# Batch normalisation after a three-tap convolution: the second batch's input transform moved between the first unit's products, with loads and last stores reordered

## Chip, cores and metric

The kernel runs on one core of a Trainium2 chip. The metric is the device time of one execution in microseconds; the median of three runs before the change is 204.71 us (204.09 to 204.76). Engines are named as the profile names them: PE is TensorE, DVE VectorE, ACT ScalarE, POOL GpSimd and SP SyncE, whose queue issues the DMAs.

## What is computed

```python
B, S, C = 2, 2048, 1024      # x is (B, S, C), w is (3, C, C), all bf16

def reference(x, w, mean, var, g, b):
    K, P = 3, 1
    xp = jnp.pad(x, ((0, 0), (P, P), (0, 0)))
    y = sum(jnp.einsum('bsc,cd->bsd', xp[:, k:k + S, :], w[k]) for k in range(K))
    inv_std = 1.0 / jnp.sqrt(var + 1e-5)
    y = (y - mean) * (g * inv_std) + b
    return jax.nn.silu(y)
```

It is a convolution over the sequence with three taps and 1024 channels in and out, then a scale and a shift for each channel and silu.

## The kernel before

**The algorithm.** Six outputs along the sequence are made from eight inputs with eight products per channel pair instead of eighteen (a Winograd form). The sequence of 2048 gives 342 tiles of six outputs (NTB). For each of the eight positions j (NJ) there is a transformed input `T_sb[bi][:, ct, j, :]` and a transformed weight; positions 0 and 7 use the raw slices w[0] and w[2], positions 1 to 6 use sums of the three slices.

**Input transform (L201 to L242).** The sequence is cut into 17 windows of 21 tiles (the last has 6), for each batch. A window's load is 256 KB (L214; the first one of a batch is two DMAs into `xw0`, L210 and L211). Eight matmuls (L224) multiply it by the small matrix `Rm`, four into each of two groups of PSUM; there are four groups of two banks, used in turn (`next_group`). Each group is evicted as bf16 into `T_sb` by ACT (L236) or DVE (L238), chosen by a running sum of costs. `Rm` is made at the start by DVE (L93) and POOL (L105). All 34 windows are done before the first product. The load of the first weights and of the parameters (L183) is issued by SP after the load of window 1; the second column block's weights are loaded after window 20, the third's after the last window.

**Weights.** For each column block dc of 128 output channels, three slices are loaded (L130), scaled by 4, 4 and 2 (L140 on DVE for the first, L142 on ACT for the others) and combined by nine POOL operations of 128x1024 (L153 to L161) into one tile `uch`. The transposed parameters `prmT` (PE L188, DVE L189) give `beta` and `sk` on POOL (L191 to L197).

**Units (L287 to L361).** A unit is one column block of one batch: 16 units. Each has 64 products (L263) of 128x128 by 128x342, eight for each of eight banks, in the order of positions 1 to 6, 0, 7. ACT copies three banks into SBUF (`Ac`, L305, L308, L309), DVE makes the sums and differences and the six outputs `y[i]` (L266, L316 to L331), ACT applies silu with scale and bias into `yT` (L296), one transposing DMA turns `yT` to rows (L340) and five stores write it (L269). Silus and stores of a unit are issued within the next unit (`late_a`, `late_b`): ACT's order is three silus, copy 0, three silus, copies 1 and 2, scalings. The last unit is transposed by PE (L356), copied by DVE and ACT (L358, L360) and stored block by block, in five stores.

**What sets the order.** The schedule is manual: on each engine instructions run in the order in which the program issues them, and an instruction that waits holds all behind it on its engine. SP issues all DMAs in one order.

Of the kernel before, what the change touches and what calls it, by code (L numbers as in the profile page):

```python
# [8 lines left out]
ACT = mybir.ActivationFunctionType  # L9
# [26 lines left out]
def kernel(  # L36
# [28 lines left out]
    upool = ctx.enter_context(tc.tile_pool(name="upool", bufs=3))  # L65
    wtmp = ctx.enter_context(tc.tile_pool(name="wtmp", bufs=1))
    pspool = ctx.enter_context(tc.tile_pool(name="ps", bufs=1, space=bass.MemoryType.PSUM))

    ps_all = pspool.tile([P, 8 * 512], FP32, name="ps_all")

    dummy = consts.tile([P, 2], FP32, name="dummy")
    nc.vector.memset(dummy, 0.0)
    nc.scalar.activation(dummy[:, 1:2], dummy[:, 0:1], ACT.Silu)

# [3 lines left out]
    nc.gpsimd.iota(val, pattern=[[-1, NJ], [-M_OUT, WT]], base=0, channel_multiplier=1)  # L78
    E = consts.tile([P, NJ, WT], FP32, name="E")
# [34 lines left out]
    xw0 = consts.tile([P, C], BF16, name="xw0")  # L114
    nc.gpsimd.memset(xw0[0:1, :], 0.0)
    ident = consts.tile([P, P], BF16, name="ident")
    make_identity(nc, ident)
# [6 lines left out]
    w_all = w.rearrange("k (ct p) d -> p k ct d", p=P)  # L124
    raw, wts = {}, {}

    def load_weights(dc):
        wch = wpool.tile([P, 3, CT, P], BF16, name="wch")
        for k in (2, 0, 1):
            nc.sync.dma_start(out=wch[:, k], in_=w_all[:, k, :, dc * P:(dc + 1) * P])  # L130
        raw[dc] = wch

    def scale_weights(dc, first=False):
        wch = raw[dc]
        w1x2 = wtmp.tile([P, CT, P], BF16, name="w1x2")
        w0x4 = wtmp.tile([P, CT, P], BF16, name="w0x4")
        w2x4 = wtmp.tile([P, CT, P], BF16, name="w2x4")
        for dst, k, f in ((w2x4, 2, 4.0), (w0x4, 0, 4.0), (w1x2, 1, 2.0)):
            if first:
                nc.vector.tensor_scalar(dst, wch[:, k], f, 0.0, op0=ALU.mult, op1=ALU.add)  # L140
            else:
                nc.scalar.mul(dst, wch[:, k], f)  # L142
        return w1x2, w0x4, w2x4

    def transform_weights(dc, scaled):
        wch = raw[dc]
        w1x2, w0x4, w2x4 = scaled
        uch = upool.tile([P, 6, CT, P], BF16, name="uch")
        e1 = wtmp.tile([P, CT, P], FP32, name="e1")
        e2 = wtmp.tile([P, CT, P], FP32, name="e2")  # L150
        eh = wtmp.tile([P, CT, P], FP32, name="eh")
        w0, w1, w2 = wch[:, 0], wch[:, 1], wch[:, 2]
        nc.gpsimd.tensor_tensor(e1, w0, w2, op=ALU.add)  # L153
        nc.gpsimd.tensor_tensor(uch[:, 0], e1, w1, op=ALU.add)  # L154
        nc.gpsimd.tensor_tensor(uch[:, 1], e1, w1, op=ALU.subtract)  # L155
        nc.gpsimd.tensor_tensor(e2, w0, w2x4, op=ALU.add)  # L156
        nc.gpsimd.tensor_tensor(uch[:, 2], e2, w1x2, op=ALU.add)  # L157
        nc.gpsimd.tensor_tensor(uch[:, 3], e2, w1x2, op=ALU.subtract)  # L158
        nc.gpsimd.tensor_tensor(eh, w0x4, w2, op=ALU.add)  # L159
        nc.gpsimd.tensor_tensor(uch[:, 4], eh, w1x2, op=ALU.add)  # L160
        nc.gpsimd.tensor_tensor(uch[:, 5], eh, w1x2, op=ALU.subtract)  # L161
        wts[dc] = (wch, uch)

    T_sb = [tpool.tile([P, CT, NJ, NTB], BF16, name=f"T_sb{bi}") for bi in range(B)]
    CH = 4
    grp_i = 0
    eng_load = {"act": 0.0, "dve": 1.0}
    EVAC_COST = {"act": 0.75, "dve": 0.80}

    def next_group():  # L170
        nonlocal grp_i
        gi = grp_i % 4
        grp_i += 1
        return ps_all[:, gi * 1024:(gi + 1) * 1024].rearrange("p (s e) -> p s e", e=256)

    prm = consts.tile([4 * DC, P], BF16, name="prm")
# [3 lines left out]

    def load_params():
        for q, ap in enumerate((var, g, mean, b)):
            nc.sync.dma_start(out=prm[q * DC:(q + 1) * DC, :], in_=ap.rearrange("(dc p) -> dc p", p=P))  # L183

    def make_params():
        grp = next_group()
        pv = grp[:, 0, 0:2 * DC].bitcast(BF16)
        nc.tensor.transpose(pv, prm, ident[0:4 * DC, 0:4 * DC])  # L188
        nc.vector.tensor_copy(prmT.rearrange("p q d -> p (q d)"), pv)  # L189
        rstd = consts.tile([P, DC], FP32, name="rstd")  # L190
        nc.gpsimd.tensor_scalar(rstd, prmT[:, 0, :], 1e-5, 1.0, op0=ALU.add, op1=ALU.mult)  # L191
        nc.gpsimd.tensor_tensor(rstd, rstd, mhalf, op=ALU.pow)
        sc = consts.tile([P, DC], FP32, name="sc")
# [5 lines left out]
    win_i = 0  # L199
    with tc.tile_pool(name="xwin", bufs=12) as xpool:  # L200
        for bi in range(B):  # L201
            for wi in range(NWIN):
                ntile = min(WT, NTB - WT * wi)
                n0 = WT * wi
                t_lo = M_OUT * n0 - 1
                t_hi = min(t_lo + M_OUT * ntile + 1, S - 1)
                kk = t_hi - t_lo + 1
                if t_lo < 0:
                    xw = xw0
                    nc.sync.dma_start(out=xw[1:113, :], in_=x[bi, 0:112, :])  # L210
                    nc.sync.dma_start(out=xw[113:kk, :], in_=x[bi, 112:t_hi + 1, :])  # L211
                else:
                    xw = xpool.tile([P, C], BF16, name="xw")
                    nc.sync.dma_start(out=xw[0:kk, :], in_=x[bi, t_lo:t_hi + 1, :])  # L214
                if win_i == 1:
                    load_weights(0)
                    load_params()
                if win_i == 20 and DC > 1:
                    load_weights(1)
                for h in range(CT // CH):  # L220
                    grp = next_group()
                    for c4 in range(CH):
                        ct = h * CH + c4
                        nc.tensor.matmul(  # L224
                            grp[:, c4, 0:NJ * ntile],
                            lhsT=xw[0:kk, ct * P:(ct + 1) * P],
                            rhs=Rm[0:kk, :, 0:ntile],
                            start=True,
                            stop=True,
                        )  # L230
                    src = grp[:, :, 0:NJ * ntile].rearrange("p s (j n) -> p s j n", j=NJ)
                    dst = T_sb[bi][:, h * CH:(h + 1) * CH, :, n0:n0 + ntile]
                    eng = min(eng_load, key=lambda e: eng_load[e] + EVAC_COST[e])
                    eng_load[eng] += EVAC_COST[eng]
                    if eng == "act":
                        nc.scalar.copy(dst, src)  # L236
                    else:
                        nc.vector.tensor_copy(dst, src)  # L238
                if win_i == 3:
                    scaled = scale_weights(0, first=True)  # L240
                    make_params()
                    transform_weights(0, scaled)  # L242
                win_i += 1
    if DC > 2:
        load_weights(2)

    epool = ctx.enter_context(tc.tile_pool(name="epool", bufs=1))
    opool = ctx.enter_context(tc.tile_pool(name="opool", bufs=2))

    out_f = out.flatten_outer_dims()  # L250
    bank = [ps_all[:, i * 512:i * 512 + NTB] for i in range(8)]


    def mms(bk, j, dc, bi):
        wch, uch = wts[dc]
        for ct in range(CT):
            if j == 0:
                lhsT = wch[:, 0, ct, :]
            elif j == 7:
                lhsT = wch[:, 2, ct, :]  # L260
            else:
                lhsT = uch[:, j - 1, ct, :]
            nc.tensor.matmul(bank[bk], lhsT=lhsT, rhs=T_sb[bi][:, ct, j, :], start=(ct == 0), stop=(ct == CT - 1))  # L263
# [4 lines left out]
    def store(dst, src):  # L268
        nc.sync.dma_start(out=dst, in_=src)  # L269

    def store_block(o_v, dc, bi, nb):
# [5 lines left out]
        cuts = [n0, n1] if (n1 - n0) % 16 == 0 else [n0, n1 - (n1 - n0) % 16, n1]  # L277
        for c0, c1 in zip(cuts, cuts[1:]):
            dst = out_f[r0 + c0 * M_OUT:r0 + c1 * M_OUT, dcols].rearrange("(n i) d -> n i d", i=M_OUT)
            store(dst, o_v[c0 - n0:c1 - n0])  # L280
        if nb == NB - 1 and S % M_OUT:
            dst = out_f[r0 + full * M_OUT:r0 + S, dcols].rearrange("(n i) d -> n i d", i=S % M_OUT)
            store(dst, o_v[full - n0:full - n0 + 1, 0:S % M_OUT])

    units = [(dc, bi) for dc in range(DC) for bi in range(B)]
    late_a, late_b = [], []
    for ui, (dc, bi) in enumerate(units):  # L287
        last = ui == len(units) - 1
        yT = yTs[ui % 2]
# [3 lines left out]
        y = [epool.tile([P, NTB], FP32, name=f"y{i}") for i in range(M_OUT)]  # L293

        def silu(i, yT=yT, y=y, dc=dc):
            nc.scalar.activation(  # L296
                yT[:, i, 0:NTB], y[i], ACT.Silu, bias=beta[:, dc:dc + 1], scale=sk[:, dc:dc + 1]
            )
# [93 lines left out]
```

## Time and profile before

| what | us |
| --- | --- |
| median of three runs | 204.71 |
| the profiled execution | 205.36 |
| its span, first to last instruction | 203.6 |
| first input matmul starts | 4.34 |
| first product starts (unit 0) | 39.82 |
| unit 1 starts on PE | 49.10 |
| last product ends | 190.95 |

Busy time of the engines in stretches of the span (core 0, us):

| stretch | PE | DVE | ACT | POOL | DMA GB/s |
| --- | --- | --- | --- | --- | --- |
| 0 to 10 | 2.99 | 4.17 | 3.62 | 4.06 | 198 |
| 10 to 20 | 9.56 | 8.97 | 7.05 | 6.25 | 329 |
| 20 to 30 | 6.84 | 7.08 | 6.44 | 9.92 | 278 |
| 30 to 40 | 9.11 | 8.96 | 8.73 | 9.84 | 288 |
| 100 to 120 | 19.80 | 18.58 | 12.97 | 19.69 | 155 |
| 190 to 204 | 3.95 | 7.13 | 4.50 | 0.00 | 117 |

Busy time is the union of an engine's instructions in the stretch. Idle time is listed with what ended it: an instruction's own releaser, taken from semaphores. A timeline row merges neighbouring instructions of one line: start, duration, engine, line, operation, output<-input, count, and in brackets the idle time before and its releaser. The chain of waits goes back from the last instruction to whatever released each one.

### The profile page before, as it was taken

To read this page: it belongs to the slowest core of one execution; us is meant where nothing else is said; L and a number is where in the kernel's file an instruction comes from. 1 tells how busy PE (TensorE), PEld (TensorE's weight loads), DVE (VectorE), ACT (ScalarE), POOL (GpSimd) and SP (SyncE) were. 2 spreads that over 40 slices of the span, in tenths; PEclk is the share of its full clock that TensorE was granted. 3 is DMA by queue.
4 is the path that set the end of the run, shared out by engine and by line. 5 is a ranking of instruction groups with operands and counts; after the bars stand their busy time and mean duration, and the time that the engine had idled before them with its cause. 6 is when DMAs were issued, how large, how long until landed. Compare 5 with 4: busy or idle time off the path is not lost.

```text
span 203.6 us, 3800 instructions
## 1 busy us (share of the span) xinstructions
PE 181.6 (89%) x1315; PEld 126.0 (62%) x1315; DVE 172.6 (85%) x386; ACT 121.1 (59%) x204; POOL 158.3 (78%) x97
## 2 busy tenths in 40 slices
PE   1499949899999999999999999999999999999550
PEld 1488739666666666666666666666666666666330
DVE  6189948839898989999998989898989999998961
ACT  2459838818738745962869096629545962719070
POOL 7039999926999999999999999999999999500000
PEclk9999987999999999999999999999999999999955
DMA  6999999800156379578976888697849665687644
GB/s 148 254 286 365 260 309 385 140 0 3 29 107 139 68 161 211 119 131 176 171 150 137 174 163 164 134 179 154 162 104 216 150 127 118 136 117 158 132 105 103
DMA packets 98455, 32.30 MB, mean 159 GB/s; under 512 B 94276, under 2 KB 94276, under 8 KB 98436
## 3 DMA queue, kind: packets, MB, share of 16 engines
q1 hardware_dynamic: 98436, 32.06, 71.6%
q8 instruction: 10, 0.16, 0.3%
q14 instruction: 9, 0.07, 0.1%
HBM read 14.82 MB, written 8.39 MB: 114 GB/s over the span
## 4 chain that ended last, share of the span: by engine, by line
DVE 36%; PE 33%; ACT 14%; issue 7%; DMA 5%; SPq 3%; DVEq 0%; ACTq 0%
PE ps_all L263 25%; DVE y L266 20%; ACT yT L296 9%; PE ps_all L224 7%; DMA xw<-in_x_dram 5%; DVE y L328 3%; DVE ps_all L318 3%; DVE T_sb L238 3%; DVE ps_all L325 2%; DVE ps_all L319 2%; DVE ps_all L324 2%; ACT Ac L305 2%; ACT Ac L308 2%; SPq L130 1%; ACT T_sb L236 1%
## 5 line engine op out<-in xcount | busy, mean ns | idle before, releaser
L263 PE MATMUL ps_all<-T_sb,uch 128*128 128x342 bf16 x768 | 115.6, 307 | 1.5 <-ACT T_sb L236 0.6
L263 PEld LDWEIGHTS <-uch 128*128 128x128 bf16 x768 | 74.3, 97 | 40.1 <-issue 3.4
L296 ACT ACTIVATE yT<-y,beta,sk 128x342 bf16<-128x342 f32 x96 | 59.3, 665 | 55.4 <-DVE y L266 51.7
L266 DVE SCALAR_TENSOR_TENSOR y<-ps_all,y 128x342 f32<-128x342 f32 x96 | 43.2, 505 | 0.5
L263 PE MATMUL ps_all<-T_sb,wch 128*128 128x342 bf16 x256 | 39.7, 308 | 0.0
L224 PE MATMUL ps_all<-Rm,xw 128*128 128x168 bf16 (+1 forms) x272 | 28.2, 265 | 10.9 <-DMA xw<-in_x_dram 5.9
L224 PEld LDWEIGHTS <-xw 128*128 128x128 bf16 (+1 forms) x272 | 24.7, 112 | 14.0 <-DMA xw<-in_x_dram 6.5
L238 DVE CAST T_sb<-ps_all 128x672 bf16<-128x672 f32 (+1 forms) x32 | 24.8, 822 | 9.6 <-PE ps_all L224 9.4
L263 PEld LDWEIGHTS <-wch 128*128 128x128 bf16 x256 | 25.0, 97 | 12.2
L236 ACT CAST T_sb<-ps_all 128x672 bf16<-128x672 f32 (+1 forms) x36 | 24.4, 723 | 13.2 <-PE ps_all L224 13.0
L266 DVE SCALAR_TENSOR_TENSOR y<-ps_all,S 128x342 f32<-128x342 f32 x48 | 21.7, 508 | 0.5
L266 DVE SCALAR_TENSOR_TENSOR y<-ps_all,D 128x342 f32<-128x342 f32 x48 | 21.5, 504 | 0.0
L156 POOL TENSOR_TENSOR e<-wch,w2x 128x1024 f32<-128x1024 bf16 x8 | 17.0, 2129 | 5.5 <-ACT w2x L142 5.5
L157 POOL TENSOR_TENSOR uch<-e,w1x 128x1024 bf16<-128x1024 f32 x8 | 17.1, 2135 | 0.6
L154 POOL TENSOR_TENSOR uch<-e,wch 128x1024 bf16<-128x1024 f32 x8 | 17.1, 2134 | 0.6
L160 POOL TENSOR_TENSOR uch<-eh,w1x 128x1024 bf16<-128x1024 f32 x8 | 17.1, 2132 | 0.6
L153 POOL TENSOR_TENSOR e<-wch 128x1024 f32<-128x1024 bf16 x8 | 17.1, 2132 | 0.4 <-DMA wch<-in_w_dram 0.4
L155 POOL TENSOR_TENSOR uch<-e,wch 128x1024 bf16<-128x1024 f32 x8 | 17.1, 2136 | 0.0
L161 POOL TENSOR_TENSOR uch<-eh,w1x 128x1024 bf16<-128x1024 f32 x8 | 17.1, 2136 | 0.0
L158 POOL TENSOR_TENSOR uch<-e,w1x 128x1024 bf16<-128x1024 f32 x8 | 17.1, 2135 | 0.0
L159 POOL TENSOR_TENSOR eh<-w0x,wch 128x1024 f32<-128x1024 bf16 x8 | 17.0, 2129 | 0.0
L318 DVE TENSOR_TENSOR ps_all<-Ac,ps_all 128x342 f32<-128x342 f32 x16 | 8.3, 520 | 7.1 <-ACT Ac L308 5.7
(46 smaller groups left out, 120.4 us busy)
## 6 DMA issues: line engine op xcount, KB each, us to landing
xw<-in_x_dram SPq DMA_DIRECT2D x30, 256.0 KB
wch<-in_w_dram SPq DMA_DIRECT2D x24, 256.0 KB
out_dram<-o_sb SPq DMA_DIRECT2D x32, 192.0 KB
out_dram<-o_sb SPq DMA_DIRECT2D x16, 120.0 KB
xw<-in_x_dram SPq DMA_DIRECT2D x2, 224.0 KB
out_dram<-o_sb SPq DMA_DIRECT2D x16, 7.5 KB
out_dram<-o_sb SPq DMA_DIRECT2D x16, 0.5 KB
o_sb<-yT SPq DMA_TRANSPOSE x15
```

Of the source, the lines that this page charges most:

```text
L153: nc.gpsimd.tensor_tensor(e1, w0, w2, op=ALU.add)
L154: nc.gpsimd.tensor_tensor(uch[:, 0], e1, w1, op=ALU.add)
L155: nc.gpsimd.tensor_tensor(uch[:, 1], e1, w1, op=ALU.subtract)
L157: nc.gpsimd.tensor_tensor(uch[:, 2], e2, w1x2, op=ALU.add)
L158: nc.gpsimd.tensor_tensor(uch[:, 3], e2, w1x2, op=ALU.subtract)
L160: nc.gpsimd.tensor_tensor(uch[:, 4], eh, w1x2, op=ALU.add)
L224: nc.tensor.matmul(grp[:, c4, 0:NJ * ntile], lhsT=xw[0:kk, ct * P:(ct + 1) * P], rhs=Rm[0:kk, :, 0:ntile], start=True, stop=True,)
L236: nc.scalar.copy(dst, src)
L238: nc.vector.tensor_copy(dst, src)
L263: nc.tensor.matmul(bank[bk], lhsT=lhsT, rhs=T_sb[bi][:, ct, j, :], start=(ct == 0), stop=(ct == CT - 1))
L266: nc.vector.scalar_tensor_tensor(out=o, in0=i0, scalar=s, in1=i1, op0=ALU.mult, op1=ALU.add)
L296: nc.scalar.activation(yT[:, i, 0:NTB], y[i], ACT.Silu, bias=beta[:, dc:dc + 1], scale=sk[:, dc:dc + 1])
```

## The change

All counts of matmuls, evictions and arithmetic stay as they are, apart from the removed running sum that chose the evicting engine. What moves:

- **Loads.** Nine windows of batch 0 and the first weights are loaded ahead (`AHEAD = 8`), weight slices between windows 2 and 5; each later window's load is issued after a window's matmuls (`next_loads`). Window buffers go from 12 to 8. The second column block's weights are loaded in unit 0, after the products of position 5.
- **Parameters.** Their four loads are issued by ACT, after the loads above in program order. Their transpose is PE's first instruction; its copy is made by ACT. Matrix `ident` and the memset of `xw0` come before POOL's part of `Rm`.
- **First unit.** Only batch 0 is transformed beforehand. In unit 0 a window of batch 1 stands before every four products, in PSUM groups 2 and 3 (banks 4 to 7), while the products use banks 0 to 3 twice. Later units use banks 4 to 7 and then 0 to 3.
- **Issue order in a unit.** Each engine's work is written after the products it needs, not after all 64.
- **Weights.** One tile for each pair of positions (`transform_pair`) instead of one for six.
- **Last stores.** The last block's stores are split between ACT's queue and SP's.

```diff
+    xpool = ctx.enter_context(tc.tile_pool(name="xwin", bufs=8))
...
+    AHEAD = 8
+    load_window(0, 0)
+    load_window(0, 1)
+    load_window(0, 2)
+    load_weights(0, (2,))
+    load_window(0, 3)
+    load_weights(0, (0,))
+    load_window(0, 4)
+    load_weights(0, (1,))
+    for wi in range(5, AHEAD + 1):
+        load_window(0, wi)
 
     dummy = consts.tile([P, 2], FP32, name="dummy")
     nc.vector.memset(dummy, 0.0)
     nc.scalar.activation(dummy[:, 1:2], dummy[:, 0:1], ACT.Silu)
+    prm = consts.tile([4 * DC, P], BF16, name="prm")
+    for q, ap in enumerate((var, g, mean, b)):
+        nc.scalar.dma_start(out=prm[q * DC:(q + 1) * DC, :], in_=ap.rearrange("(dc p) -> dc p", p=P))
...
+    def transform_pair(dc, pair, scaled=None):
+        w0, w1, w2 = (raw[dc][:, k] for k in range(3))
...
+        u = upool.tile([P, 2, CT, P], BF16, name="u")
+        e = wtmp.tile([P, CT, P], FP32, name="e")
+        nc.gpsimd.tensor_tensor(e, s0, s2, op=ALU.add)
+        nc.gpsimd.tensor_tensor(u[:, 0], e, s1, op=ALU.add)
+        nc.gpsimd.tensor_tensor(u[:, 1], e, s1, op=ALU.subtract)
...
+    def window(bi, wi, gis, engs):
+        xw, kk, ntile = xw_of[bi, wi]
+        n0 = WT * wi
+        for h in range(CT // CH):
+            grp = group(gis[h])
+            for c4 in range(CH):
...
+            if engs[h] == "act":
+                nc.scalar.copy(dst, src)
+            else:
+                nc.vector.tensor_copy(dst, src)
...
+    pv = group(3)[:, 0, 0:2 * DC].bitcast(BF16)
+    nc.tensor.transpose(pv, prm, ident[0:4 * DC, 0:4 * DC])
+    nc.scalar.copy(prmT.rearrange("p q d -> p (q d)"), pv)
+    make_params()
+    for wi in range(NWIN):
+        window(0, wi, ((2 * wi) % 4, (2 * wi + 1) % 4), ("act", "dve"))
+        if wi > 0:
+            next_loads()
+        if wi == 3:
+            transform_pair(0, 1)
+        if wi == 4:
+            scaled = scale_weights(0, first=True)
+            transform_pair(0, 2, scaled)
+            transform_pair(0, 3, scaled)
...
+    BANKS = (4, 5, 6, 7, 0, 1, 2, 3)
+    BANKS_FIRST = (0, 1, 2, 3, 0, 1, 2, 3)
...
+        def next_window():
+            if first and B > 1 and nwin1[0] < NWIN:
+                k = nwin1[0]
+                window(1, k, (2, 3), ("act", "act" if k % 6 == 5 else "dve"))
+                nwin1[0] += 1
+                next_loads()
+
+        def mms(bk, j):
+            for ct in range(CT):
+                if ct % 4 == 0:
+                    next_window()
+                nc.tensor.matmul(
+                    bank[bk], lhsT=lhs(dc, j, ct), rhs=T_sb[bi][:, ct, j, :], start=(ct == 0), stop=(ct == CT - 1)
+                )
+
+        mms(0, 1)
+        if prev:
+            finish(prev, (2, 4, 0))
         nc.scalar.copy(Ac[0], bank[0])
+        mms(1, 2)
...
+        mms(2, 3)
+        if prev:
+            finish(prev, (1, 3, 5))
+            write_out(prev)
+        nc.scalar.copy(Ac[1], bank[2])
+        mms(3, 4)
         nc.vector.tensor_tensor(bank[2], Ac[1], bank[3], op=ALU.subtract)
         nc.vector.tensor_tensor(bank[3], Ac[1], bank[3], op=ALU.add)
+        mms(4, 5)
+        nc.scalar.copy(Ac[2], bank[4])
         for i in (0, 2, 4):
             stt(y[i], bank[3], ALPHA * 2.0 ** i, S1)
         for i in (1, 3, 5):
             stt(y[i], bank[2], ALPHA * 2.0 ** i, D1)
+        if bi == 0 and dc + 1 < DC:
+            if dc == 0:
+                load_weights(1)
+            scaled = scale_weights(dc + 1)
+            transform_pair(dc + 1, 1)
+            transform_pair(dc + 1, 2, scaled)
+            transform_pair(dc + 1, 3, scaled)
+        if bi == 0 and dc + 2 < DC:
+            load_weights(dc + 2)
+        mms(5, 6)
...
+        mms(6, 0)
...
+        mms(7, 7)
+        if first:
+            while B > 1 and nwin1[0] < NWIN:
+                next_window()
...
+        store_block(o_sb[:, :, nb, :], dc, bi, nb, [nc.sync] if nb < 2 else [nc.scalar, nc.sync])
```

The functions `load_window` and `load_weights` issue the DMAs of L210 to L214 and L130 as before, on SP; `finish` issues the silus of L296 and `write_out` the transposing DMA and the stores of a unit. In `store_block` the stores of a block go to the listed queues in turn.

## The prediction

> **What bounds the kernel now.** I read the page's busy table, the chain that ended last, the timeline of each engine up to 42 us, and SyncE's own waits, in this order.
>
> ```profile
> span 203.6 us, 3800 instructions
> PE 181.6 (89%) x1315; PEld 126.0 (62%) x1315; DVE 172.6 (85%) x386; ACT 121.1 (59%) x204; POOL 158.3 (78%) x97
> ```
>
> No engine is full over the span. The chain, in order of time, says what turns in a unit:
>
> ```profile
> 109.07 0.42 ACT Ac L305
> 109.49 0.90 ACT yT L296 x2
> ...
> 110.53 0.66 ACT yT L296
> 111.19 0.34 ACT Ac L308
> 111.55 0.52 DVE ps_all L318
> ...
> 117.48 0.53 DVE y L328
> 118.06 0.56 issue
> 118.61 0.42 ACT Ac L305
> ```
>
> This is a loop of ACT and DVE: first copy, three silus of the unit before, second copy, DVE from L318 to L328, one silu (the piece called issue), and the next first copy. It turns in 118.61 - 109.07 = 9.54 us. PE needs less: 64 products, 9.29 us from 39.82 to 49.10 in its timeline. L318 stands at 54.27 in unit 1 and at 187.93 in unit 15, 14 turns of 9.547 us, and the span ends 15.7 us after that. So whatever moves unit 1's L318 moves the end by as much, if the loop stays. Before the loop:
>
> ```profile
> 9.41 2.42 PE L224 MATMUL ps_all<-Rm,xw 128*128 128x168 bf16 x16 [2.67 <-DMA xw<-in_x_dram]
> 12.35 13.75 PE L224 MATMUL ps_all<-Rm,xw 128*128 128x168 bf16 x136 [0.39 <-DMA xw<-in_x_dram]
> 28.90 10.28 PE L224 MATMUL ps_all<-Rm,xw 128*128 128x168 bf16 x104 [2.80 <-DMA xw<-in_x_dram]
> 39.82 2.48 PE L263 MATMUL ps_all<-T_sb,uch 128*128 128x342 bf16 x16 [0.64 <-ACT T_sb L236]
> 15.37 8.33 DVE L238 CAST T_sb<-ps_all 128x672 bf16<-128x672 f32 x11 [0.19 <-PE ps_all L224]
> 15.93 7.04 ACT L236 CAST T_sb<-ps_all 128x672 bf16<-128x672 f32 x11 [0.39 <-PE ps_all L224]
> ```
>
> With data there, a window takes what DVE needs for one half: 8.33/11 = 0.76 us (ACT 0.64). PE's own part is 0.58 us (0.0725 per matmul, from neighbouring starts). After the idle 2.80 us the matmuls stand 0.14 us apart for 3.4 us and the granted clock of 28.90 to 32.87 is 0.57; the first four windows, 4.34 to about 15.7, run at that pace too. Batch 0 takes until about 22.5, batch 1 until 39.5.
>
> **The change, part by part.** Counts of matmuls, evictions, weight and output instructions are the same (36 halves on ACT, 32 on DVE, both ways). Per unit, the order within ACT and within DVE is the old one, so the loop keeps 9.547 us; other banks and the split weight tiles cost nothing. Moving mask and memset on POOL ahead of the selects makes Rm about 1.4 us later (0.94 + 0.49, from 3.25 to 4.7), hidden behind the wait of the next step. Were that cover gone, it would cost 0.4, as DVE's share of Rm ends at 4.29 anyway.
>
> *Parameters first.* PE's first instruction is now the transpose of prm, and prm comes by four DMAs on ACT's queue, the 14th to 17th of the program. SyncE's waits show what a late DMA does:
>
> ```profile
> SPq L214 <- DMA xw<-in_x_dram: 3.9, 13, 0.6
> SPq L130 <- DMA xw<-in_x_dram: 2.2, 5, 0.9
> SPq L214 <- DMA wch<-in_w_dram: 0.4, 1, 0.4
> ```
>
> The load held 0.4 us by a weight slice is that of window 5, issued at 8.33. It has a buffer nobody used and shares no data with the slice; but the slice is the eighth DMA before it. Counted so, every issue waits until the eighth DMA before it has landed. I take it to hold across queues. Then the last parameter load, the 17th, waits in ACT's queue for the 9th, the last weight slice. Before, windows 0 and 1 and three slices had landed by 8.3 us; now windows 2, 3 and 4 are ahead of that slice as well, 3 x 0.8 us (262 KB at the 329 GB/s of 10 to 20 us): 10.7. Issue 0.7 (dearest row of a parameter load, 0.73; the others 0.3) and 1.7 us to landing (the last 0.5 KB store, issued at 201.01, is waited for until 202.7) give 13.1 for PE's start; ends 12.3 and 14.5. Queued behind it: on PE every window, on ACT all evictions, on SyncE from window 9 on the loads that need window 1's buffer (SyncE itself sheds the four parameter issues, 4.86 to 6.60 before; the loads behind them gain 1.7 us that nobody waits for). From 13.1, three windows at the slow pace (3.4 us) bring 16.5; DVE sets the rest: from its cast of window 3 at 17.0, 13 halves x 0.76 = 9.9, three scalings of the first weights now in the midst of it (1.25; before they fell into a slow stretch), 0.3 for the short window: 28.4. PE, two halves ahead of DVE, begins batch 1 at **27.55** (before: 22.9). POOL's weights of the first unit are ready as before: parameters 13.4 to 16.4, pairs at 22.8, 29.2 and 35.6, each ahead of its products below.
>
> *Batch 1 between the products.* Each window has one left and one right half instead of four groups. A half can be written again only after its eviction: 0.22 (first to last matmul) + 0.30 (to the cast) + 0.86 + 0.05 = 1.43 us on DVE, 1.30 on ACT; PE with four products (0.58) and eight matmuls (0.58) would need 1.16. So 1.43 a window: window 8 is written 8 x 1.43 + 0.6 = 12.0 us after the start. Then two queues stand in the way, in program order:
> - DVE has six sums of 0.42 us between its casts of windows 9 and 10; window 10's is over at 18.0.
> - ACT has three scalings of the next weights ahead of its half of window 10, and those weights are loaded only now: their issue stands in SyncE behind the load of the last window, which waits for window 8's buffer. The three slices of before went out at 2.12 and had landed at 8.3, 6.2 us with two windows ahead of them; a run of three issues alone takes 4.19 (at 32.15). I take 5.2 from first issue to last landing (ends 4.2 and 7). With 0.45 to get there, the second scaling starts at 12.0 + 5.7 = 17.7, both end at 19.6, the eviction frees its half at 20.4.
>
> PE has then stood since 15.1, 5.3 us, longer than the 2.8 us after which the clock was low for 3.4 us; window 11 and four products at double time cost 1.0 more. Product six is complete at 22.8; five DVE operations (2.1) stand before window 12's cast at 24.9; the next four windows take 1.43 each: PE ends the first unit at **30.2** after its start (ends 28.3, no wait for weights and no slow clock, and 32). Before, batch 1 and unit 0 together took 49.10 - 22.92 = 26.2.
>
> Weights for unit 2: POOL starts them at 27.55 + 16.9 = 44.4, third pair ready at about 63.6; unit 2 starts at 67. No stall; its 19.2 us per column block then run beside 19.1.
>
> *Last stores.* The 480-row store goes to ACT at about 199.2 instead of 199.42; the short ones no longer stand in one queue, so the end waits for the 480 rows (202.1 before) instead of the last store (202.7): -0.7, ends -0.3 and -1.2. [...]
>
> **The sum.** Unit 1 starts at 27.55 + 30.2 = 57.75, its L318 at 4.9 after (unit 0 before: 44.73 - 39.82) = 62.65, against 54.27: +8.4. With the stores +7.7. The profiled execution took 205.36 us (1.76 around its span), so 213.0 for its like; the median of the runs is 204.71, which makes **212.4 us**. [...]
>
> **Rivals.**
> - *Parameters do not wait their turn* (the count of eight is SyncE's alone). For it: no DMA on ACT is in this trace. Against: a landing is what is counted, and that is no queue's own. PE starts at about 6; then the loads pace batch 0: 10.7 for the last weight slice, 11.3 windows after it x 0.8 and 1.2 for the last one's matmuls and evictions bring batch 1 to 20.9, 6.65 earlier: 205.75 us, with the first unit's ends 203.9 to 207.6. It decides if PE's first window begins before 8.
> - *Batch 1 does hide in the first unit*: the faster side. Place: the left and right halves of the first unit. For it: DVE's own work there is only 15 x 0.76 + 24 x 0.42 = 21.5 us, ACT's 17. Against: both are strictly in order and a half has no second buffer. At PE's sum, 9.29 + 17 x 0.58 = 18.7 instead of 30.2, with the late parameters: 212.4 - 11.5 = 200.9 us. It decides where the unit takes under 22.5 us.
> - *A longer stall*: the scaled weights land 4 us later still, or POOL then falls behind in the later blocks: 216.4 us. Against: eight-deep loading and the 3 us in hand above.
>
> **Numbers.** Forecast 0.70, parameters without a turn 0.16, hidden 0.08, longer stall 0.06. The time is the forecast's, 212.4, its own range by the ends above (-0.8, -1.9, -0.5 and +1.4, +1.8, +0.4) 209.2 to 216.0. To hold 8 in 10 the range goes down over most of the first rival and up to 216: 205 to 216. A measurement of this kernel tells about 0.3% (0.6 us) from no change. Faster: the hidden case and the lower tail of the first rival, 0.12; same 0.05; slower 0.83.
>
> **What would show it.** PE's first matmul is the transpose at 12 to 14.5 us with ACT's DMA issues waiting on landings just before; the first window at 6 refutes that. Right-half casts in the first unit 1.4 us apart; one idle of 4 to 6 us on PE in it, with ACT waiting on the weights' DMA; a low clock after it. Units from the second on at 9.55 us. I am wrong altogether if the first unit takes under 23 us or if the loop's turn has changed.

## The result, and the profile after

The changed kernel takes 217.58 us (median of four runs, 216.70 to 218.23); the kernel before took 204.50 beside it (204.09 to 204.76). The ratio is 1.0639 [1.0590, 1.0688]: slower, as forecast, but by 13.1 us and not by the 7.7 of the sum, and above the end of the range, 216.

The page of the changed kernel (its profiled execution took 218.23 us) begins:

```profile
span 216.4 us, 3802 instructions
PE 183.0 (85%) x1315; PEld 126.2 (58%) x1315; DVE 179.6 (83%) x385; ACT 122.1 (56%) x205; POOL 159.5 (74%) x97
```

The same matmuls, in a span 12.8 us longer. DVE is busy 7.0 us more than before with one instruction less: something on DVE has become longer, which is the first thing to look for. The loop that sets the pace from unit 1 on is not it. The chain of waits in the middle of the span (start, duration, what):

```profile
120.43 0.42 ACT Ac L341
120.86 0.90 ACT yT L296 x2
...
122.56 0.34 ACT Ac L349
122.92 0.52 DVE ps_all L351
...
128.85 0.53 DVE y L376
...
129.42 0.56 issue
129.98 0.42 ACT Ac L341
```

The links are the same and the turn is 129.98 - 120.43 = 9.55 us; 14 turns, from 65.42 to 199.28, take 133.86 us (before 133.66). So the time went before and after the loop. The same view from its start:

```profile
1.72 3.90 DMA xw<-in_x_dram
6.06 4.75 DMA xw<-in_x_dram
10.86 0.77 PE ps_all L224 x8
11.65 0.86 DVE T_sb L236
12.51 2.30 DVE w2x L176
14.80 2.26 DVE w1x L176
17.07 2.25 DVE w0x L176
19.32 0.78 DVE T_sb L236
20.14 5.21 PE ps_all L224 x36
...
40.70 0.46 PE ps_all L224 x4
41.97 0.57 SPq L99
42.59 5.01 DMA wch<-in_w_dram
47.68 1.06 ACT w1x L178
48.74 0.95 ACT w0x L178
49.68 0.66 ACT T_sb L234
50.38 1.28 PE ps_all L224 x8
```

Two blocks stand out. Three scalings of the first weights on DVE are the chain from 12.51 to 19.32, and then 36 matmuls take 5.21 us, 0.145 each, at a granted clock of 0.50 (20.1 to 25.2). And between 40.70 and 50.38 the chain goes through the issue and landing of a weight slice, ACT's scalings and ACT's eviction. The timeline shows what stands beside them (in brackets the idle time before and what ended it):

```profile
0.91 0.61 ACTq L118 DMA_DIRECT2D prm<-in_var_dram  x1
5.17 0.18 PE L247 MATMUL ps_all<-ident,prm 32*128 32x32 bf16 x1 [5.17 <-POOL yT L166]
12.39 2.13 POOL L192 TENSOR_TENSOR u<-e,wch 128x1024 bf16<-128x1024 f32 x1
12.42 2.38 DVE L176 TENSOR_SCALAR w2x<-wch 128x1024 bf16<-128x1024 bf16 x1
14.47 2.30 POOL L193 TENSOR_TENSOR u<-e,wch 128x1024 bf16<-128x1024 f32 x1
14.72 2.34 DVE L176 TENSOR_SCALAR w1x<-wch 128x1024 bf16<-128x1024 bf16 x1
20.14 9.66 PE L224 MATMUL ps_all<-Rm,xw 128*128 128x168 bf16 x84 [5.20 <-DVE T_sb L236]
50.38 1.28 PE L224 MATMUL ps_all<-Rm,xw 128*128 128x168 bf16 x8 [5.37 <-ACT T_sb L234]
```

The parameters' loads went out from 0.91 on and waited for nothing; PE's transpose runs at 5.17. A scaling took 0.42 us before the change, and POOL stood idle beside it, waiting for the parameters:

```profile
12.08 0.42 DVE L140 TENSOR_SCALAR w2x<-wch 128x1024 bf16<-128x1024 bf16 x1
13.35 0.20 POOL L191 TENSOR_SCALAR rstd<-prmT 128x8 f32<-128x8 f32 x1 [8.17 <-DVE prmT L189]
```

It takes 2.38 now, beside a POOL operation, and ends each time 0.3 us after a POOL operation has ended (14.80 and 14.52, 17.06 and 16.77). PE stands 5.20 us the first time and 5.37 us the second. Two rows of SyncE's waits (total, times, longest) after the change:

```profile
SPq L99 <- DMA xw<-in_x_dram: 2.0, 2, 1.2
...
SPq L287 <- DMA out_dram<-o_sb: 2.7, 1, 2.7
```

Two of the first weight slices now wait for the landing of windows (before, in SyncE's first 10 us, nothing but one window's load waited for a landing, 0.4 us; the prediction's row of 2.2 us belongs to later slices), and one of the last stores waits for that of another store, which is new. Stage by stage, in span time (us):

| stage | before | forecast | after |
| --- | --- | --- | --- |
| batch 1's first window on PE | 22.92 | 27.55 | 28.79 |
| from there to unit 1 on PE | 26.18 | 30.2 | 31.72 |
| from there to the first difference of unit 1 (L318, now L351) | 5.17 | 4.9 | 4.91 |
| 14 turns of the loop | 133.66 | 133.66 | 133.86 |
| from the last of them to the end | 15.64 | 14.94 | 17.14 |
| span | 203.6 | 211.3 | 216.4 |

Against the forecast: 1.24 + 1.52 + 0.01 + 0.20 + 2.20 = 5.17 us. The 1.24 hides two larger errors of opposite sign, as the experiments show.

### The profile page after: what moved, and what is told of

Read it like the earlier page. It is cut to its first block, busy times and chain, and to the rows that moved or that the text cites. A ratio compares the mean times of both kernels' runs of the same rounds, so it can differ in the third digit from the quotient of the medians.

```text
span 216.4 us, 3802 instructions
## 1 busy us (share of the span) xinstructions
PE 183.0 (85%) x1315; PEld 126.2 (58%) x1315; DVE 179.6 (83%) x385; ACT 122.1 (56%) x205; POOL 159.5 (74%) x97
## 4 chain that ended last, share of the span: by engine, by line
DVE 54%; ACT 16%; PE 10%; issue 9%; DMA 6%; SPq 1%; DVEq 0%; ACTq 0%
DVE y L275 27%; ACT yT L296 10%; DVE T_sb L236 6%; PE ps_all L224 6%; DMA xw<-in_x_dram 4%; DVE y L376 4%; DVE ps_all L351 4%; PE ps_all L334 3%; DVE ps_all L370 3%; DVE ps_all L369 3%; DVE ps_all L352 3%; ACT Ac L341 3%; DMA wch<-in_w_dram 2%; ACT Ac L349 2%; DVE w2x L176 1%
## 5 line engine op out<-in xcount | busy, mean ns | idle before, releaser
L334 PE MATMUL ps_all<-T_sb,u 128*128 128x342 bf16 x768 | 118.0, 308 | 0.9
L334 PEld LDWEIGHTS <-u 128*128 128x128 bf16 x768 | 74.2, 97 | 38.5 <-issue 2.7
L296 ACT ACTIVATE yT<-y,beta,sk 128x342 bf16<-128x342 f32 x96 | 59.3, 666 | 53.6 <-DVE y L275 50.0
L224 PE MATMUL ps_all<-Rm,xw 128*128 128x168 bf16 (+1 forms) x272 | 30.9, 264 | 16.2 <-DVE T_sb L236 6.7
L334 PE MATMUL ps_all<-T_sb,wch 128*128 128x342 bf16 x256 | 40.8, 311 | 0.0
L192 POOL TENSOR_TENSOR u<-e,w1x 128x1024 bf16<-128x1024 f32 x16 | 34.2, 2135 | 1.3
L236 DVE CAST T_sb<-ps_all 128x672 bf16<-128x672 f32 (+1 forms) x32 | 25.8, 824 | 10.8 <-PE ps_all L224 10.6
L193 POOL TENSOR_TENSOR u<-e,w1x 128x1024 bf16<-128x1024 f32 x16 | 34.1, 2133 | 0.0
L191 POOL TENSOR_TENSOR e<-wch 128x1024 f32<-128x1024 bf16 x8 | 17.0, 2126 | 18.7 <-DMA wch<-in_w_dram 18.3
L192 POOL TENSOR_TENSOR u<-e,wch 128x1024 bf16<-128x1024 f32 x8 | 17.0, 2130 | 0.6
L191 POOL TENSOR_TENSOR e<-w0x,wch 128x1024 f32<-128x1024 bf16 x8 | 17.0, 2126 | 0.6
L193 POOL TENSOR_TENSOR u<-e,wch 128x1024 bf16<-128x1024 f32 x8 | 17.2, 2154 | 0.0
L351 DVE TENSOR_TENSOR ps_all<-Ac,ps_all 128x342 f32<-128x342 f32 x16 | 8.3, 519 | 6.7 <-ACT Ac L349 5.1
L369 DVE TENSOR_TENSOR ps_all<-Ac,ps_all 128x342 f32<-128x342 f32 x16 | 8.2, 510 | 5.7 <-PE ps_all L334 5.7
L385 DVE TENSOR_TENSOR y<-ps_all,y 128x342 f32<-128x342 f32 x16 | 8.2, 515 | 2.0 <-DVE y L275 0.5
```

Source lines behind the costliest of these rows:

```text
L191: nc.gpsimd.tensor_tensor(e, s0, s2, op=ALU.add)
L192: nc.gpsimd.tensor_tensor(u[:, 0], e, s1, op=ALU.add)
L193: nc.gpsimd.tensor_tensor(u[:, 1], e, s1, op=ALU.subtract)
L224: nc.tensor.matmul(grp[:, c4, 0:NJ * ntile], lhsT=xw[0:kk, ct * P:(ct + 1) * P], rhs=Rm[0:kk, :, 0:ntile], start=True, stop=True,)
L296: nc.scalar.activation(yT[:, i, 0:NTB], y[i], ACT.Silu, bias=beta[:, dc:dc + 1], scale=sk[:, dc:dc + 1])
L334: nc.tensor.matmul(bank[bk], lhsT=lhs(dc, j, ct), rhs=T_sb[bi][:, ct, j, :], start=(ct == 0), stop=(ct == CT - 1))
```

## Experiments

Each run is compared with runs of the kernel before on the same chip in the same batch; the ratio to them, with its 95% interval, is what compares between batches. Edits are to the changed kernel. The start of batch 1, the first unit and the end are read from the trace of each. Kernels that share the changed kernel's start (the two on the last stores and on batch 1 ahead, and the one with earlier weights) began batch 1 at 27.6 to 27.8; the profiled execution of the changed kernel, at 28.79, was its slowest of four, so about 1 us of its start is spread.

### The first scalings on ACT

```diff
-            if first:
-                nc.vector.tensor_scalar(dst, wch[:, k], f, 0.0, op0=ALU.mult, op1=ALU.add)
-            else:
-                nc.scalar.mul(dst, wch[:, k], f)
+            nc.scalar.mul(dst, wch[:, k], f)
```

> The three scalings of the first weights move from DVE to ACT; nothing else changes. Theory (DVE's scalings, 2.34 to 2.38 us each, are held by POOL's running operation and hold the casts behind them): DVE casts of windows 4 to 6 follow at once, PE's idle 5.20 us goes, and the first product comes at 23.5 to 25 us instead of 29.6; ACT pays 3 x 1.05 us. Time 212 to 213.5. Rival (the scalings were long because their weights landed late): ACT waits as long, its evictions stand behind it, and the time stays within 1 us of 217.6.

212.25 us (four runs), 1.0374 [1.0282, 1.0467]. Batch 1 starts at 22.61, 6.2 us earlier than in the changed kernel.

```profile
11.75 1.05 ACT L175 ACTIVATE w2x<-wch 128x1024 bf16<-128x1024 bf16 x1
11.85 2.13 POOL L189 TENSOR_TENSOR u<-e,wch 128x1024 bf16<-128x1024 f32 x1
...
15.36 8.26 PE L221 MATMUL ps_all<-Rm,xw 128*128 128x168 bf16 x88 [1.46 <-ACT T_sb L231]
```

The weights had landed (the scaling starts at 11.75 with no wait for a DMA), and ACT's 1.05 us stands beside a POOL operation of the usual 2.13 without lengthening either. PE's idle shrinks from 5.20 to 1.46, and the matmuls after it run at 8.26/88 = 0.094 us each, where the 36 after the idle 5.20 us ran at 0.145. So the price of those three instructions being on DVE at that time is 6.2 us, or 5.1 against the starts of 27.6 to 27.8 named above. It doesn't say yet why.

### The same scalings with two inputs on DVE

```diff
-                nc.vector.tensor_scalar(dst, wch[:, k], f, 0.0, op0=ALU.mult, op1=ALU.add)
+                nc.vector.scalar_tensor_tensor(out=dst, in0=wch[:, k], scalar=f - 1.0, in1=wch[:, k], op0=ALU.mult, op1=ALU.add)
```

> The three scalings stay on DVE, at the same place and with the same waits, but as a two-input operation (3w + w, or w + w). Theory (only the one-input bf16 form waits for POOL's operation to end): 1.0 to 1.2 us each, some 3.7 us less in all, first product at about 26, time about 214. Rival (any DVE operation beside POOL's is slowed alike, or the weights are late): again 2.3 us each, time 217.6.

219.29 us (four runs), 1.0712 [1.0621, 1.0802]; batch 1 at 29.65. The form with two inputs waits as well:

```profile
11.23 2.12 POOL L192 TENSOR_TENSOR u<-e,wch 128x1024 bf16<-128x1024 f32 x1
11.29 3.13 DVE L176 SCALAR_TENSOR_TENSOR w2x<-wch 128x1024 bf16<-128x1024 bf16 x1
...
13.30 3.10 POOL L193 TENSOR_TENSOR u<-e,wch 128x1024 bf16<-128x1024 f32 x1
...
14.35 3.14 DVE L176 SCALAR_TENSOR_TENSOR w1x<-wch 128x1024 bf16<-128x1024 bf16 x1
```

DVE's starts at 11.29 and ends at 14.42, which is 1.07 after the POOL operation's end at 13.35; POOL's next one begins at 13.30 and ends at 16.40, which is 1.98 after DVE's end. The two take turns, and each stands for all of the other's instruction. That only the form with one input is held fell here; that the two engines exclude each other is confirmed on both sides.

### POOL kept idle while DVE scales

```diff
-        for dst, k, f in ((w2x4, 2, 4.0), (w1x2, 1, 2.0), (w0x4, 0, 4.0)):
+        for dst, k, f in ((w1x2, 1, 2.0), (w0x4, 0, 4.0), (w2x4, 2, 4.0)):
...
-        if wi == 3:
-            transform_pair(0, 1)
...
             transform_pair(0, 2, scaled)
+            transform_pair(0, 1)
             transform_pair(0, 3, scaled)
```

> The changed kernel with its first scalings on DVE in the same form, but POOL's first operation needs the last of the three, so that POOL stands still while they run. Theory (DVE's scaling and POOL's operation exclude one another): 0.42 us each, as before the change, the first product at 23.5 to 25, time 212 to 213.5. Rival (scalings at this place are slow for another reason, such as the arriving weights): 2.3 us each, 217.6 or more.

212.79 us (two runs), 1.0392 [1.0336, 1.0448]; batch 1 at 22.49.

```profile
11.81 0.42 DVE L176 TENSOR_SCALAR w1x<-wch 128x1024 bf16<-128x1024 bf16 x1
12.14 0.42 DVE L176 TENSOR_SCALAR w0x<-wch 128x1024 bf16<-128x1024 bf16 x1
12.47 0.42 DVE L176 TENSOR_SCALAR w2x<-wch 128x1024 bf16<-128x1024 bf16 x1
12.98 2.12 POOL L191 TENSOR_TENSOR e<-wch,w2x 128x1024 f32<-128x1024 bf16 x1 [4.56 <-DVE w2x L176]
```

Same engine, same instructions, same place on DVE; only POOL stands still, because its first operation needs the last scaling. 0.42 us each, as before the change. This is the direct test: it is POOL's running operation that the scalings waited for.

### The last stores on one queue

```diff
-        store_block(o_sb[:, :, nb, :], dc, bi, nb, [nc.sync] if nb < 2 else [nc.scalar, nc.sync])
+        store_block(o_sb[:, :, nb, :], dc, bi, nb, [nc.sync])
```

> All last stores on SP's queue again. Theory (the 30-row store on SP stands 2.7 us until the 480-row store on ACT has landed, since both use one landing semaphore): the end comes 15.7 us after the last unit's L351 instead of 17.1, time 216.1. Rival (two queues do save issue time and the longer end has another cause): the end comes 0.5 to 1 us later still, time 218.3.

215.51 us (four runs), 1.0515 [1.0413, 1.0618]. From the last L351 to the end it takes 15.6 us again, 1.5 less than with two queues; the row of 2.7 us on `out_dram` in SyncE's waits is gone. The run with the scalings on ACT, which has two queues, has that row of 2.7 us too; the interleaving with its other faults mended, which has one queue, does not have it, and the kernel before, with one queue, takes 15.6 us for its end as well. The rest of this run's lead over the changed kernel is its earlier start of batch 1.

### Batch 1 ahead of unit 0

All 17 windows of batch 1 before the first product, on four groups as in the kernel before; unit 0 keeps its four banks.

```diff
+    for wi in range(NWIN):
+        window(1, wi, ((2 * wi + 2) % 4, (2 * wi + 3) % 4), ("act", "act" if wi % 6 == 5 else "dve"))
+        next_loads()
...
-    nwin1 = [0]
+    nwin1 = [NWIN]
```

> All windows of batch 1 are transformed before unit 0, in four groups in turn, and unit 0 runs without them; the rest is the changed kernel. Theory (a half without a second buffer, and ACT's and DVE's other work in its way, make the first unit 31.7 us long): 17 x 0.76 and 9.3 us take 22.5, unit 1 starts at 51.2 instead of 60.5, time 208.5. Rival (interleaving itself costs nothing, all is lost before the first product): 217 or more.

209.32 us (four runs), 1.0234 [1.0128, 1.0340]. Batch 1 and unit 0 take 51.46 - 27.82 = 23.64 us, where the interleaving took 31.72. So the interleaving is worth -8.1 us, not a gain. The second block's weights, still loaded at the same place of the program, cost nothing here: with all windows ahead their loads went out from 35.29 on, and ACT scaled them from 46.93 on without a wait.

### The second block's weights earlier

```diff
...
             next_loads()
+        if wi == 14:
+            load_weights(1)
...
-            if dc == 0:
-                load_weights(1)
```

> The second column block's weights are loaded after window 14 of batch 0 instead of within unit 0; nothing else changes. Theory (in unit 0 ACT's scalings wait for these weights, and its half of window 10 stands behind them): no wait of ACT on a weights' DMA, PE's idle in unit 0 falls from 5.4 to about 2.5 us (the scalings themselves remain), unit 0 with batch 1 takes 28.5 to 29.5 instead of 31.7 us, time 214.5 to 215.5. Rival (the stall is the scalings' own time and DVE's block of six sums): within 1 us of 217.6.

213.94 us (four runs), 1.0420 [1.0336, 1.0504]. The first unit with batch 1 takes 56.01 - 27.58 = 28.43 us, and the stall in it is half:

```profile
46.45 0.74 PE L224 MATMUL ps_all<-Rm,xw 128*128 128x168 bf16 x8 [2.63 <-ACT T_sb L234]
47.02 1.28 PE L336 MATMUL ps_all<-T_sb,u 128*128 128x342 bf16 x4
```

What remains, 2.63 us, is three scalings of 1.05 that stand in ACT's order ahead of an eviction. Of the interleaving's 8.1 us the late weights are 31.72 - 28.43 = 3.3, and 28.43 - 23.64 = 4.8 are left with the weights there: the pace of the windows, the scalings and DVE's sums ahead of evictions.

### The interleaving with its other faults mended

The scalings on ACT, the stores on one queue and the weights early: three of the edits above together.

> The changed kernel's interleaving as it is, with first scalings on ACT, second block's weights loaded after window 14 and last stores on SP. Theory (the halves' turn of 1.43 us and DVE's blocks of sums remain): batch 1 and unit 0 take 28 to 29 us from 22.6, unit 1 at 51, time 206 to 207.5. Rival (the waits were the whole price of interleaving): 24 us or less, unit 1 by 47, time 202.5.

207.19 us (ten runs), 1.0148 [1.0100, 1.0197]: still slower than before, by 1.5%. Batch 1 starts at 21.95, 1.0 us earlier than before the change, and the first unit takes 27.60 (before 26.18). The profiled execution, 205.54, was the fastest of the ten, and its span, 203.7, is that of before; so the trace shows the longer first unit, but not the whole 1.5%.

### Batch 1 ahead with the same faults mended

The scalings on ACT, the stores on one queue, batch 1 ahead, and eight banks for unit 0 as well.

```diff
...
-        bank = [ps_all[:, i * 512:i * 512 + NTB] for i in (BANKS_FIRST if first else BANKS)]
+        bank = [ps_all[:, i * 512:i * 512 + NTB] for i in BANKS]
...
```

> All batch 1 windows before unit 0, first scalings on ACT, last stores on SP, unit 0 on eight banks. Theory (the three prices add up: 6.2, 9 to 10.5 and 1.45 us): batch 1 starts at 22.6, unit 1 at 44.8, time 200 to 201, below the kernel before. Rival (they overlap, or the loads of batch 1 set the pace once nothing else does): unit 1 at 48 or later, time 204 or more.

201.56 us (four runs), 0.9827 [0.9743, 0.9910]: faster than both kernels, by 1.7% against the one before. Batch 1 and unit 0 take 46.36 - 24.09 = 22.27 us, 1.4 less than with four banks, where PE waited 1.43 us for DVE to give a bank free. The start of batch 1 came 1.5 later than in the other runs with the scalings on ACT, so unit 1 began at 46.36 where 44.8 was expected (the profiled execution, 202.60, is 2.2 above the fastest of the four; in it the granted clock was between 0.5 and 0.6 in the profile's slice from 15.1 to 20.1, where it was 0.9 or more in the run above). This run and the one above have the same runs of before beside them and differ, but for the place of one weight load, in the interleaving and the banks it takes: 27.60 against 22.27 in the first unit, 207.19 against 201.56 in time. That is the price of the interleaving with its four banks: 5.3 us by the traces, 5.6 by the medians, 6.6 by the ratios.

### Half of the windows ahead, the rest spaced out

Eight windows ahead; nine in unit 0, one before every eight products; the scalings, on ACT, spread over the unit; the stores on one queue and the weights early.

```diff
...
-                if ct % 4 == 0:
+                if ct == 0:
                     next_window()
...
```

> Eight batch 1 windows before unit 0 in four groups, the other nine within it, one before every eight products; first scalings on ACT, weights of the second block loaded ahead, their three scalings spread over unit 0, last stores on SP. Theory (a half costs 1.43 us on DVE; with eight products beside it PE needs 1.74, so the evictions hide): 8 x 0.76 + 9 x 1.74 = 21.7 us, unit 1 at 43.5 to 45, time 199 to 201. Rival (interleaving costs in any dose, by the queues' order): unit 1 at 48 or later, 204 or more.

202.63 us (four runs), 0.9872 [0.9811, 0.9934]: 1.3% faster than before, but unit 1 starts at 47.14 and not at 43.5 to 45.

```profile
31.54 1.32 PE L336 MATMUL ps_all<-T_sb,u 128*128 128x342 bf16 x8
...
33.28 1.32 PE L336 MATMUL ps_all<-T_sb,u 128*128 128x342 bf16 x8
...
41.91 0.45 PE L221 MATMUL ps_all<-Rm,xw 128*128 128x168 bf16 x4 [1.27 <-DVE T_sb L233]
...
44.91 0.45 PE L221 MATMUL ps_all<-Rm,xw 128*128 128x168 bf16 x4 [1.10 <-DVE T_sb L233]
```

A window and eight products take 1.74 us on PE, more than the 1.43 that one pair of halves needs, so the windows do hide as long as DVE is free. They stop hiding where DVE's blocks of sums stand ahead of its cast: six sums from 38.49 to 41.09, the cast from 41.01, and PE goes on at 41.91.

### Most windows ahead

Thirteen ahead, four in the first four positions of unit 0, which has eight banks; the scalings on ACT, the stores on one queue; the next weights are loaded after the third window of batch 1.

> Thirteen batch 1 windows before unit 0, the other four one before each of its first four products, that is, before DVE's blocks of sums; first scalings on ACT, second block's weights loaded ahead, last stores on SP, eight banks. Theory (a window beside eight products costs 0.58 us of PE as long as DVE has only casts): 13 x 0.76 + 9.3 + 3.3 x 0.58 = 21.1 us, unit 1 at 43.7 to 45, time 199 to 200.5, below the version with all windows ahead. Rival (loads or evictions of batch 1 set the pace, interleaved or not): unit 1 at 46 or later, 201 or more.

206.43 us (seven runs), 1.0086 [1.0051, 1.0121]: a miss. Unit 1 starts at 48.67.

```profile
33.63 2.28 PE L221 MATMUL ps_all<-Rm,xw 128*128 128x168 bf16 x16 [2.33 <-DMA xw<-in_x_dram]
36.33 1.16 PE L221 MATMUL ps_all<-Rm,xw 128*128 128x168 bf16 x8 [0.41 <-ACT T_sb L231]
```

With the windows ahead, PE catches up with the loads: from 25.66 to 28.60 three weight slices go out between the windows in SyncE's queue, PE waits 2.33 us for a window's load, and the next three windows run at a granted clock of 0.58 (33.6 to 35.0) and 0.52 (35.0 to 37.3), the first two at 2.28/16 = 0.14 us a matmul, twice the 0.0725 at which the kernel before runs with data there. In the run with all windows ahead, where the slices come behind the last window, PE has no such wait. The four interleaved windows themselves stood 1.74 us apart, hidden. How this order would do with loads further ahead was not tried.

## Why the prediction was right and wrong

**Right.** The loop keeps its turn, 9.55 us. Batch 1 does not hide in the first unit: right-half casts stand 1.40 us apart (29.83, 31.23, 32.63, 34.04; forecast 1.43), PE stands 5.37 us (5.3), ended by ACT's eviction behind scalings that waited for their weights, and the granted clock is 0.50 from 50.3 to 55.2. The unit takes 31.72 us against 30.2, inside its ends; 0.9 of the difference is the weights' landing, 47.68 - 41.54 = 6.1 us from the first issue to the last slice instead of 5.2. (The second rival's sum, 9.29 + 17 x 0.58, is 19.15 and not 18.7; its time would be 0.4 us later, which changes nothing.)

**Wrong: "Parameters first".** The count of eight held, and it holds across queues; the step that failed is the one that gives out the turns in the order of the program. In the trace the 159 DMAs of SyncE and ACT raise eight semaphores, 101 and 103 to 109, each of them 19 or 20 times. The first eight to use them were four loads of windows 0 to 2 and ACT's four parameter loads, though these come 14th to 17th in the program; the first weight slice, fifth in the program, was the ninth: it raises 101 again, waited for window 0, which had raised 101 first, and went out at 3.44. So it is the slices that waited, 2.0 us, and PE's first window began at 5.30 where 13.1 was forecast. The first rival's sign, a start before 8, came true, and so did what it says of the parameters, that they do not wait; its reason, a count that is SyncE's alone, did not.

**Wrong: the three scalings "now in the midst of it (1.25)".** They took 7.05 us, with PE idle for 5.20, and the low clock after it: which is 6.2 us of the start of batch 1 against the run with them on ACT and 6.3 against the run with POOL idle (by the ratios, 1.0639 - 1.0374 and 1.0639 - 1.0392, 5.4 and 5.1 us of the time: about 1 us less, the spread of the start). The sum priced them by rows in which POOL happened to be idle (12.08 to 13.17 before the change, ahead of POOL's first operation on the parameters at 13.35). In the changed kernel POOL has the parameters behind it at 8.61, and the first pair needs no scaled weight, so POOL runs when DVE scales. That was to be seen in the forecast's own times: there too POOL's first pair, 16.4 to 22.8, runs beside the scalings. This error of +5.8 and the parameters' error of about -5 nearly cancelled: batch 1 was forecast at 27.55 and came at 27.6 to 28.8; that they agree is luck. It is also why the first rival's 205.75 us didn't come, and without the exclusion its start of batch 1, 20.9, was still 1.6 too early (22.5 and 22.6 in the two runs).

**Wrong: "Last stores", -0.7.** They cost 1.50. The step let the short stores on SyncE go at once. In the trace the 30-row store on SyncE and the 480-row store on ACT raise the same semaphore, 108, and SyncE, whose issue before ends at 210.72, waits for 108 until 213.43: the 30-row store goes out at 213.46, when the 480 rows have landed:

```profile
210.57 0.73 ACTq L287 DMA_DIRECT2D out_dram<-o_sb  x1
213.46 0.83 SPq L287 DMA_DIRECT2D out_dram<-o_sb  x1
```

In the kernel before, on one queue, the five last stores raise five different ones, 104 to 108, and none is held by another. Why the program gave these two the same is not shown.

With these three in place the sum closes: the first rival's 205.75, + 1.6 (its start), + 6.2 (scalings), + 1.5 (first unit), + 2.2 (stores), + 0.2 (loop) = 217.5 us, against 217.6. Its terms are differences between the traces, so this shows that no term of size is missing and is no test of the causes.

## What to carry to other kernels

Before an instruction is moved, look at which engine was idle beside it in the row that gives its price: a VectorE scaling that took 0.42 us beside an idle GpSimd took 2.33 to 2.38 beside a busy one. Give work that is to hide between products a spacing wider than its buffer's turn (here eight products and a window, 1.74 us of PE, hid; four and a window, 1.16 us, did not and went at the buffer's 1.40; a second buffer would be another way, not tried here) and no long block of another kind ahead of its evictions on either engine (six sums, 38.49 to 41.09, cost PE 1.27 us); otherwise run it ahead on all banks, which took 22.27 us for batch 1 and the first unit here instead of 27.60. Before a second DMA queue is used, see whether its transfers share a completion semaphore with the first: here two stores shared 108, and the end came 1.5 us later; look for the wait in the queue's own rows.

## What had not been expected of the hardware

In these runs DVE's scalings and POOL's operations of 128x1024 excluded each other for whole instructions: a scaling took 0.42 us alone, 2.33 to 2.38 beside POOL's operations of 2.12 to 2.30; with two inputs 3.13, and then POOL's own grew to 2.97 to 3.10. ACT's scaling took 1.05 us beside a busy POOL and 1.06 beside an idle one (38.47 in the run with half of the windows ahead), and POOL's 2.13 beside it stayed as it was; DVE's evictions from PSUM took the same 0.86 us beside a busy POOL (11.65 in the changed kernel) as beside an idle one (10.26 in the kernel before). What in the engines makes the two take turns is not shown.

In these runs the length of an idle stretch alone didn't tell if PE's clock fell. After 2.63 us the granted clock stayed at 1.00 in the mended interleaving (38.0 to 46.5), and after the same 2.63 us with only the weights early it was 0.77 from 46 to 48 and 0.50 from 48 to 50; after 2.33 us in the run with most windows ahead it was 0.58 and 0.52. With batch 1 ahead and the same faults mended it was between 0.5 and 0.6 from 15.1 to 20.1, though PE had stood no longer than 1.35 us at a time since its first window.
